# Three weight units of the first MLP, narrowed over six items instead of three

## The chip, the cores and the metric

One core of a Trainium2 chip runs the kernel. The metric is the device time of one execution in microseconds (us). The engines are TensorE (PE, matmuls), VectorE (DVE), ScalarE (ACT), GpSimd (POOL) and SyncE (SP, which here issues most of the DMAs). Each engine works through its own queue in the order in which the program was written.

## The reference

Pooled attention feeds an MLP with squared ReLU, whose result is routed to the best of eight experts. The change lies in the first MLP.

```python
q_pool = q.reshape(B, H, S // 2, 2, D).mean(axis=3)
attn = softmax(scale * q_pool @ k.T); attn_out = attn @ v     # 2 x 8 heads, 1152 keys, D = 64
x = attn_out.transpose(0, 2, 1, 3).reshape(1152, 512)
h = x @ w_in                      # 512 x 2048, float64 weights
r = np.maximum(h, 0.0)
x = (r * r) @ w_out               # 2048 x 512, float64 weights
...                               # gate, top 1 of 8 experts, capacity 288: relu(x @ w1[e]) @ w2[e]
```

## The kernel before

**The MLP.** The 1152 tokens are cut into 3 blocks of 384 (`tb`) and the 2048 hidden columns into 2 halves (`hf`) of 8 blocks of 128 (`f`). An *item* is one `(hf, tb, f)`; there are 48, numbered from 0, in that order of loops. `g1` of an item makes the first product into a bank `bs` (L939, 12 matmuls: four blocks of the 512 inputs times three products of high and low parts), ACT makes `r` from it with Relu (L948) and the high part `gh` of its square (L950), DVE squares `r` (L952) and subtracts `gh` to get the low part `gl` (L954). `g2` makes the second product from these (L968, 9 matmuls: three blocks of 128 tokens, each with `gh` times the high weights, `gh` times the low weights, `gl` times the high weights). PE does `g1` of item n and then `g2` of item n - 2. The first product of item 0 is already made at the end of the attention stage. From item to item two `bs` banks, two `r` buffers and three pairs `gh`, `gl` take turns.

**The weights.** They arrive as float64. One *unit* is 256 hidden columns, of `w_in` or of `w_out`, so each unit serves two values of `f`. Eight pairs make 16 units; those numbered 0 to 7 are of the first half `hf`: units 0, 2, 4, 6 are `w_in` and 1, 3, 5, 7 are `w_out`. A unit is loaded raw (`ops[0]`, 1 MB, L157 or L162), narrowed to float32 by three DVE instructions of 128 x 1024 each on its bits (L171, L177, L183), and then split: a high part is copied out (L206 on POOL or L204 on ACT) and DVE subtracts it to make the low part (L210 of `split_lo`). There are two raw buffers: unit 6 has one to itself, units 5 and 7 share the other, so the load of unit 7 waits until L183 of unit 5 has read it. Units 0 to 4 are made during the attention stage, the last of them on POOL (L206 and L210) just as the items begin. Units 5, 6 and 7 are made beside the first items. Their users are `g2` of item 4 for unit 5, `g1` of item 6 for unit 6, and `g2` of item 6 for unit 7.

**The order around the items.** The kernel is scheduled by hand: an engine's queue has the order of the code. `mat(n, f, front)` puts a piece of work beside item n. In item n the program writes `g1` of item n, then the work of front 1, then `g2` of item n - 2 (from n = 2 on), then the work of front 2 (the default) and 3. The work at n = -1 comes before item 0.

```python
    for n in range(NI):
        g1(*items[n])
        for f in mtodo.pop((n, 1), []):
            f()
        if 2 <= n < NI - 1:
            g2(*items[n - 2])
        for x in (2, 3):
            for f in mtodo.pop((n, x), []):
                f()
```

In the kernel before, unit 5 is narrowed beside item 0, unit 6 beside item 1 and unit 7 beside item 2, and each is split at the next item's front 1.

Of the kernel before, what the change touches and what calls it, by code (L numbers as in the profile page):

```python
# [21 lines left out]
def tile_pooled_attention__relu2_mlp__top1_experts(  # L22
# [122 lines left out]
    wf = {}  # L145
# [54 lines left out]
    def split_hi(key, src, eng_hi="pool"):  # L200
        hi, lo = slots.take(), slots.take()
        halves[key] = (hi, lo)
        if eng_hi == "act":
            nc.scalar.activation(out=hi, in_=src, func=AF.Copy)  # L204
        else:
            nc.gpsimd.tensor_scalar(out=hi, in0=src, scalar1=1.0, scalar2=0.0, op0=ALU.mult, op1=ALU.add)  # L206

    def split_lo(key, src, eng=None, hold=False):
        hi, lo = halves[key]
        (eng or nc.vector).tensor_tensor(out=lo, in0=src, in1=hi.bitcast(F32), op=ALU.subtract)  # L210
        if not hold:
            stage.give(src)

    def split(key, src, eng_hi="pool", eng_lo=None, hold=False):
        split_hi(key, src, eng_hi)
        split_lo(key, src, eng_lo, hold)
# [11 lines left out]
    pool = att.enter_context(tc.tile_pool(name="scores", bufs=1, space=PSUM))  # L228
# [293 lines left out]
    for w in range(5):  # L522
        ops = nwork.pop(0)
# [460 lines left out]
    def mat(n, f, front=2):  # L984
        mtodo.setdefault((n, front), []).append(f)
# [2 lines left out]
    PB = NTB * FH  # L988
    for w, key in enumerate(units[5:8]):
        ops = nwork.pop(0)  # L990
        mat(-1 if w < 2 else 0, ops[0])
        for u, f in enumerate(ops[1:]):
            mat(w, f, 1 + (u == 2))
        mat(w + 1, lambda key=key, w=w: split(key, wf[key], "act" if w == 1 else "pool"), 1)
    assert KX >= 2 * XTW
    grow = [af[:, KU + i * UW : KU + (i + 1) * UW] for i in range(NGROW)]
    early = 7
# [11 lines left out]
    for j in range(HI):  # L1009
        for u, kind in enumerate(("in", "out")):  # L1010
            key = (kind, HI + j)
# [416 lines left out]
```

## Time and profile before

| | us |
|---|---|
| median of 3 runs | 596.58 (596.32 to 598.05) |
| profiled execution, its own time | 597.89 |
| its span, first to last instruction | 596.1 |
| PE busy | 572.1 (96%) |
| DVE busy | 338.7 (57%) |
| ACT busy | 260.8 (44%) |
| POOL busy | 168.7 (28%) |

The busy times are sums over the whole span; the stages differ, so what matters for a change in one stage is the stretch in which it lies. The attention stage ends at about 234 us, the items run from there to about 440 us, the experts follow.

### The profile page before, as it was taken

How to read it: one execution, taken by the hardware profiler on the slowest of the kernel's cores; microseconds unless marked ns; L12 is line 12 of the kernel's file. 1: busy time of each engine (PE TensorE's matmuls, PEld its weight loads, DVE VectorE, ACT ScalarE, POOL GpSimd, SP SyncE). 2: the span in 40 equal slices, each digit the busy share in tenths (PEclk: the TensorE clock that was granted, in tenths of full speed). 3: DMA queues.
4: the chain of work that ended last, by engine and by line, in shares of the span. 5: the costliest groups of instructions: out<-in, count | busy, mean ns of one | idle time of the engine just before them, and what ended most of it. 6: DMA issues, size and time to landing. Idle time of an engine off the chain costs nothing. (4 is left out here: it accounts for less than half of the span.)

```text
span 596.1 us, 13050 instructions
## 1 busy us (share of the span) xinstructions
PE 572.1 (96%) x5309; PEld 443.1 (74%) x5309; DVE 338.7 (57%) x550; ACT 260.8 (44%) x552; POOL 168.7 (28%) x274
## 2 busy tenths in 40 slices
PE   8999999999999999889999999999998997989994
PEld 4788889888888878778989999888886453444342
DVE  4889798888888784956569932335354110111110
ACT  5787878787877765223232322323432111010110
POOL 3746457575636253300014200001022121000011
PEclk9999999999999999999999999999999998999998
DMA  8674964417343003121344780001066940999400
GB/s 203 186 232 149 313 222 150 108 55 196 79 120 112 3 6 139 70 73 73 140 141 134 264 308 1 0 2 45 0 232 244 286 110 23 378 346 361 159 8 15
DMA packets 37639, 84.72 MB, mean 142 GB/s; under 512 B 4225, under 2 KB 8837, under 8 KB 37568
## 3 DMA queue, kind: packets, MB, share of 16 engines
q1 hardware_dynamic: 35824, 80.71, 42.3%
q0 software_dynamic: 1376, 2.81, 1.3%
q8 instruction: 47, 0.77, 0.5%
q10 hardware_dynamic: 368, 0.23, 0.2%
q14 instruction: 24, 0.20, 0.1%
HBM read 73.83 MB, written 11.37 MB: 143 GB/s over the span
## 5 line engine op out<-in xcount | busy, mean ns | idle before, releaser
L939 PE MATMUL bs<-ax,gs 128*128 128x384 f32 x564 | 107.1, 338 | 0.4 <-ACT af L496 0.4
L376 DVE TENSOR_REDUCE nm<-sc 128x1 f32<-128x1152 f32 x72 | 97.3, 1354 | 11.3 <-ACT af L437 4.0
L939 PEld LDWEIGHTS bs<-ax,gs 128*128 128x128 f32 x564 | 99.7, 188 | 5.2 <-issue 1.2
L968 PE MATMUL bt<-gs,gg 128*128 128x512 f32 x360 | 94.1, 397 | 3.4 <-DVE gg L954 3.4
L367 PE MATMUL sc<-gs 64*128 64x384 f32 x576 | 94.3, 363 | 0.0
L384 ACT ACTIVATE af<-sc,nm 128x1152 f32<-128x1152 f32 x72 | 87.7, 1218 | 9.7 <-DVE nm L376 9.4
L968 PEld LDWEIGHTS bt<-gs,gg 128*128 128x128 f32 x360 | 66.4, 188 | 16.9 <-DVE gg L954 4.7
L948 ACT ACTIVATE af<-bs 128x384 f32<-128x384 f32 x47 | 23.1, 492 | 120.7 <-PE bs L939 117.6
L367 PEld LDWEIGHTS sc<-gs 64*128 64x128 f32 x576 | 65.0, 187 | 7.3 <-issue 3.4
L952 DVE TENSOR_TENSOR af<-af 128x384 f32<-128x384 f32 x48 | 28.5, 593 | 72.6 <-ACT af L948 71.9
L411 PE MATMUL bm<-ident,af 64*128 64x64 f32 x576 | 50.5, 226 | 1.0 <-DVE af L435 0.5
L411 PE MATMUL ba<-ident,af 64*128 64x64 f32 x576 | 49.9, 227 | 0.6 <-DVE af L435 0.3
L411 PEld LDWEIGHTS bm<-ident,af 64*128 64x128 f32 x576 | 43.2, 138 | 9.3 <-DVE af L435 4.1
L206 POOL TENSOR_SCALAR gs<-af 128x1024 fp32r<-128x1024 f32 x15 | 20.2, 1347 | 85.6 <-PE bs L939 66.2
L435 DVE COPY af<-bm 128x512 f32<-128x512 f32 x56 | 38.2, 682 | 10.1 <-PE ba L411 7.7
L411 PEld LDWEIGHTS ba<-ident,af 64*128 64x128 f32 x576 | 41.3, 139 | 1.5 <-DVE af L435 0.6
L437 ACT ACTIVATE af<-ba 128x512 f32<-128x512 f32 x56 | 33.3, 595 | 20.0 <-PE ba L411 15.3
L738 POOL DMA_INDIRECT disp<-af,rslot x9 | 9.2, 1018 | 95.3 <-DVE rslot L900 60.8
L473 PE MATMUL ba<-af,gx 128*64 128x128 f32 x576 | 35.0, 275 | 0.7 <-ACT af L437 0.6
L473 PEld LDWEIGHTS ba<-af,gx 128*64 128x64 f32 x576 | 31.1, 137 | 5.6 <-ACT af L437 3.6
L473 PE MATMUL ba<-af 128*64 128x128 f32 x576 | 35.0, 275 | 0.1
L473 PEld LDWEIGHTS ba<-af 128*64 128x64 f32 x576 | 31.1, 137 | 5.0 <-ACT af L437 3.0
(208 smaller groups left out, 850.0 us busy)
## 6 DMA issues: line engine op xcount, KB each, us to landing
af<-in_moe_w_dram SPq DMA_DIRECT2D x32, 512.0 KB, 8.2
gf<-in_moe_w_dram SPq DMA_DIRECT2D x30, 512.0 KB, 7.4
af<-in_moe_w_in_dram SPq DMA_DIRECT2D x8, 1024.0 KB, 5.4
af<-in_moe_w_out_dram SPq DMA_DIRECT2D x8, 1024.0 KB, 4.9
af<-in_q_dram SPq DMA_DIRECT2D x28, 288.0 KB, 4.8
disp<-af SPq DMA_DIRECT2D x6, 771.0 KB, 6.9
af<-in_k_dram SPq DMA_DIRECT2D x12, 192.0 KB, 4.2
af<-in_v_dram SPq DMA_DIRECT2D x4, 576.0 KB, 5.4
```

Source lines behind the costliest of these rows:

```text
L206: nc.gpsimd.tensor_scalar(out=hi, in0=src, scalar1=1.0, scalar2=0.0, op0=ALU.mult, op1=ALU.add)
L367: inst = nc.tensor.matmul(S_[part_, bank, :KS], lhsT=lhs[rows2[r]], rhs=rhs[rows2[r], kc], start=(m == 0), stop=(m == len(groups_) - 1),)
L376: inst = nc.vector.tensor_reduce(out=nm, in_=bank_sets[n % 2][:, :, :KS], axis=AX.XY, op=ALU.max, negate=True)
L384: inst = nc.scalar.activation(out=prs[n % NPB].rearrange("p (i s) -> p i s", i=3), in_=bank_sets[n % 2][:, :, :KS], func=AF.Exp, bias=st.p ...
L411: nc.tensor.transpose(views[:, m, :], x, ident[rows2[i], rows2[i]])
L435: nc.vector.tensor_copy(out=dst, in_=src)
L437: nc.scalar.activation(out=dst, in_=src, func=AF.Copy)
L473: inst = nc.tensor.matmul(av[rows2[h], :w], lhsT=vs[p % 2][:, h, c * D : (c + 1) * D], rhs=of(c, h), start=(c == 0), stop=(c == NKC - 1),)
L939: nc.tensor.matmul(ph[:, :TB], lhsT=w[:, cw], rhs=x[:, d, tb * TB : (tb + 1) * TB], start=(n == 0), stop=(n == 3 * NDC - 1),)
L948: nc.scalar.activation(out=r, in_=ph[:, :TB], func=AF.Relu)
L952: nc.vector.tensor_tensor(out=g, in0=r, in1=r, op=ALU.mult)
L968: nc.tensor.matmul(accs[tb][t], lhsT=g[:, ct], rhs=w[:, cw], start=(f == 0 and n == 0), stop=(f == FH - 1 and n == 2),)
```

## The change

The loop over units 5, 6 and 7 (`w` = 0, 1, 2) places its pieces elsewhere.

```diff
     for w, key in enumerate(units[5:8]):
         ops = nwork.pop(0)
-        mat(-1 if w < 2 else 0, ops[0])
         for u, f in enumerate(ops[1:]):
-            mat(w, f, 1 + (u == 2))
-        mat(w + 1, lambda key=key, w=w: split(key, wf[key], "act" if w == 1 else "pool"), 1)
+            mat(2 * w + (u > 0), f, 1 + (u == 2))
+        mat(-1 if w < 2 else 1, ops[0])
+        mat(2 * w + 2, lambda key=key: split(key, wf[key], "act"))
```

Each unit now has two items: L171 beside the first, L177 and L183 beside the second, and the split after that, at front 2 of items 2, 4 and 6. The load of unit 7 is written at item 1, behind L183 of unit 5, instead of at item 0. All three high parts are made on ACT (L204); before, units 5 and 7 had theirs on POOL (L206). The queue of SP and the order of PE's instructions are the same as before.

On DVE, at the beginning of the items, the queue before reads as follows, from the low part of item 0 (`gg` holds `gh` and `gl`, `af` holds raw and narrowed weights and `r`, `gs` the split weights).

```order
L954 TENSOR_TENSOR gg<-af,gg 128x384
L171 TENSOR_SCALAR af<-af 128x1024
L177 SCALAR_TENSOR_TENSOR af<-af 128x1024
L183 SCALAR_TENSOR_TENSOR af<-af 128x1024
L952 TENSOR_TENSOR af<-af 128x384
L954 TENSOR_TENSOR gg<-af,gg 128x384
L210 TENSOR_TENSOR gs_75<-af,gs_75 128x1024
L171 TENSOR_SCALAR af<-af 128x1024
L177 SCALAR_TENSOR_TENSOR af<-af 128x1024
L183 SCALAR_TENSOR_TENSOR af<-af 128x1024
L952 TENSOR_TENSOR af<-af 128x384
L954 TENSOR_TENSOR gg<-af,gg 128x384
```

A whole unit stands ahead of L952 and L954 of each item. In the changed kernel, from the same place:

```order
L954 TENSOR_TENSOR gg<-af,gg 128x384
L171 TENSOR_SCALAR af<-af 128x1024
L952 TENSOR_TENSOR af<-af 128x384
L954 TENSOR_TENSOR gg<-af,gg 128x384
L177 SCALAR_TENSOR_TENSOR af<-af 128x1024
L183 SCALAR_TENSOR_TENSOR af<-af 128x1024
L952 TENSOR_TENSOR af<-af 128x384
L954 TENSOR_TENSOR gg<-af,gg 128x384
L171 TENSOR_SCALAR af<-af 128x1024
L210 TENSOR_TENSOR gs_75<-af,gs_75 128x1024
L952 TENSOR_TENSOR af<-af 128x384
L954 TENSOR_TENSOR gg<-af,gg 128x384
```

L952 and L954 of item 1 now have one instruction of unit 5 ahead of them instead of three, and L171 of the next unit stands ahead of L210 of the one before.

On ACT the difference between the two kernels is this piece of the queue, from item 2 on (its Relu from the second `bs` bank, L948, and its square, L950, come first).

```order
 L948 ACTIVATE af<-bs_3879 128x384
 L950 ACTIVATE gg<-af 128x384
-L948 ACTIVATE af<-bs_3878 128x384
-L950 ACTIVATE gg<-af 128x384
-L948 ACTIVATE af<-bs_3879 128x384
-L950 ACTIVATE gg<-af 128x384
+L204 ACTIVATE gs_75<-af 128x1024
+L948 ACTIVATE af<-bs_3878 128x384
+L950 ACTIVATE gg<-af 128x384
+L948 ACTIVATE af<-bs_3879 128x384
+L950 ACTIVATE gg<-af 128x384
+L204 ACTIVATE gs_75<-af 128x1024
```

Ahead of this piece one L204 stands in both kernels, behind item 2: of unit 6 before, of unit 5 in the changed kernel. The two that are added stand behind item 4 and behind item 6.

## Rows read from the trace of the kernel before

**Rows 1.** Windows: length, busy us by engine (instructions), PE clock, DMA share, GB/s.

```profile
230.00:260.00 30.00, 25.61 (x195) 22.67 (x192) 23.96 (x28) 8.59 (x20) 11.31 (x18) 1.00 0.19 60
260.00:300.00 40.00, 40.00 (x201) 36.04 (x200) 23.18 (x32) 11.79 (x23) 0.00 (x0) 1.00 0.25 89
```

**Rows 2.** PE's waits from 225 us on: total us, times, longest.

```profile
PE bt L968 <- DVE gg L954: 3.4, 3, 1.7
PE bt L1165 <- PEq L1302: 2.4, 1, 2.4
```

**Rows 3.** Timeline of PE: start, us, what, idle before.

```profile
240.99 2.27 PE L939 MATMUL bs<-ax,gs 128*128 128x384 f32 x12
243.10 0.63 PE L968 MATMUL bt<-gs,gg 128*128 128x512 f32 x2
244.56 1.91 PE L968 MATMUL bt<-gs,gg 128*128 128x512 f32 x7 [0.83 <-DVE gg L954]
246.31 2.25 PE L939 MATMUL bs<-ax,gs 128*128 128x384 f32 x12
...
251.69 2.26 PE L939 MATMUL bs<-ax,gs 128*128 128x384 f32 x12
...
257.81 2.25 PE L939 MATMUL bs<-ax,gs 128*128 128x384 f32 x12
...
282.99 2.27 PE L939 MATMUL bs<-ax,gs 128*128 128x384 f32 x12
```

**Rows 4.** Timeline of DVE beside the first items.

```profile
236.85 0.82 DVE L171 TENSOR_SCALAR af<-af 128x1024 uint32<-128x1024 uint32 x1
...
239.68 2.91 DVE L183 SCALAR_TENSOR_TENSOR af<-af 128x1024 uint32<-128x1024 uint32 x1
...
243.25 1.25 DVE L954 TENSOR_TENSOR gg<-af,gg 128x384 fp32r<-128x384 f32 x1
...
249.34 0.56 DVE L954 TENSOR_TENSOR gg<-af,gg 128x384 fp32r<-128x384 f32 x1
249.89 1.23 DVE L210 TENSOR_TENSOR gs<-af,gs 128x1024 fp32r<-128x1024 f32 x1
251.03 0.69 DVE L171 TENSOR_SCALAR af<-af 128x1024 uint32<-128x1024 uint32 x1
251.75 1.23 DVE L177 SCALAR_TENSOR_TENSOR af<-af 128x1024 uint32<-128x1024 uint32 x1
253.01 1.23 DVE L183 SCALAR_TENSOR_TENSOR af<-af 128x1024 uint32<-128x1024 uint32 x1
254.16 0.55 DVE L952 TENSOR_TENSOR af<-af 128x384 f32<-128x384 f32 x1
254.84 1.18 DVE L954 TENSOR_TENSOR gg<-af,gg 128x384 fp32r<-128x384 f32 x1
```

**Rows 5.** Timeline of ACT: the one high part that it makes.

```profile
248.80 1.06 ACT L204 ACTIVATE gs<-af 128x1024 fp32r<-128x1024 f32 x1 [8.64 <-DVE af L183]
```

**Rows 6.** Timeline of POOL; last, line 210 alone: ns shortest/median/longest.

```profile
237.09 1.49 POOL L206 TENSOR_SCALAR gs<-af 128x1024 fp32r<-128x1024 f32 x1
238.66 2.85 POOL L210 TENSOR_TENSOR gs<-af,gs 128x1024 fp32r<-128x1024 f32 x1
...
243.06 1.04 POOL L206 TENSOR_SCALAR gs<-af 128x1024 fp32r<-128x1024 f32 x1
254.40 1.22 POOL L206 TENSOR_SCALAR gs<-af 128x1024 fp32r<-128x1024 f32 x1 [10.30 <-DVE af L183]
...
L210 POOL TENSOR_TENSOR gs<-af,gs x5: 1996/2000/2847, 93.9 to 238.7; 128x1024 fp32r<-128x1024 f32 x5
```

**Rows 7.** Load of unit 7 on SP; DMA issues 215 to 300 us: KB, landing.

```profile
242.62 0.37 SPq L162 DMA_DIRECT2D af<-in_moe_w_out_dram  x1
...
af<-in_moe_w_out_dram SPq DMA_DIRECT2D x4, 1024.0 KB, 4.9
```

**Rows 8.** Window behind the branch of L1302, columns as in group 1.

```profile
502.37:509.00 6.63, 6.52 (x14) 3.60 (x15) 0.00 (x0) 1.07 (x2) 0.00 (x0) 0.50 0.39 126
```

## The prediction

> **What bounds the kernel now.** I read the windows first. From 260 us on PE is busy for all of its 40.00 us and VectorE (DVE) for 23.18 of them, so PE is the bound there; from 230 to 260 us PE is busy for 25.61 of 30 us and DVE for 23.96 [rows 1]. This second stretch holds the first MLP items. PE's waits come next. From 225 us to the end the largest is 3.4 us in three pieces, always the second product (L968) waiting for `gl`, the low part that DVE makes at L954; no DMA is among PE's longer waits, so what PE gains in the MLP should reach the end [rows 2].
>
> PE's own timeline gives the price. An undisturbed item takes 4.197 us: item 6 begins at 257.81 and item 12 at 282.99, 25.18 us for six. The first product of item 3 begins at 240.99 and that of item 6 at 257.81, 16.82 us where three items should take 12.59 [rows 3]. So **4.23 us** are lost, 0.81 more than the 3.42 us of bare gaps (three times 0.27 us for getting under way again).
>
> DVE's rows tell why. One unit costs DVE, from start to start, 0.72 (L171), 1.26 (L177), 1.15 (L183) and 1.14 (L210), 4.27 us, and one item 0.68 (L952) plus 0.55 (L954), 1.23 us [rows 4]. A unit in every item is 5.5 us against PE's 4.2: the queue of DVE falls behind. POOL adds to it. L183 at 239.68 took 2.91 us beside POOL's L210, while it takes 1.23 at 253.01; L954 at 254.84 took 1.18 [rows 4, 6].
>
> **The change, step by step.** It adds no arithmetic. Two high parts go from POOL's L206 (1.04 us) to ScalarE's L204 (1.06 us) [rows 5, 6]; ACT is busy for 8.59 of the 30 us [rows 1], so both are covered there. The 12 DVE instructions of the units stay and are spread: 4.27 + 2 x 1.23 = 6.73 us for two items against 8.39 us of PE. That removes the backlog, if the order meets PE's due times. I place them with item k's first product at 240.99 + 4.197 (k - 3) and the second product that follows 2.11 us later (243.10 - 240.99) [rows 3]; its third matmul, which reads `gl`, about 0.5 us on.
>
> *Item 1.* L171 begins at 236.85 as before. L952 and L954 of item 1 now come right behind it, but POOL works for the earlier unit at that time: L206 from 237.09 to 238.58, then L210 to 241.51 [rows 6]. Unhindered, they are done at 236.85 + 0.72 + 0.68 + 0.55 = 238.8. At the other end each waits for POOL: L183 ended 1.08 us after POOL's L210 (242.59 against 241.51) [rows 4, 6], which gives 242.6. I take a point between: L954 at 243.25 ended 0.40 us after L206 on POOL did (244.50 against 244.10) [rows 4, 6], so L952 ends at 238.98, POOL's L210 then runs its usual 2.00 us to 240.98, L954 ends at 241.4. PE wants this `gl` at 243.6: met in all three cases.
>
> [...]
>
> *The tight place.* Behind L954 of item 1, DVE works through L177, L183, item 2, L171 of the second unit, L210 of the first, item 3, L177, L183, item 4, L171 of the third unit, and then L210 of the second: 2 x 1.26 + 2 x 1.15 + 3 x (0.68 + 0.55) + 2 x 0.72 + 1.14 = 11.09 us, and 1.23 for that last L210 itself [rows 4]. From 241.4 it is done at 253.7. Its low part is a weight of item 6, whose first product begins at 240.99 + 12.59 = 253.58 and reads it in its third matmul, two twelfths of 2.11 us later, at 253.93. So it is 0.2 us early; from 238.8 it is 2.8 us early, from 242.6 it is 1.0 us late and costs 1.0 + 0.27 = 1.3 us. I take no stall, the price by the middle.
>
> *The rest is not tight.* `gl` of items 2, 3 and 4 comes at about 245.1, 248.1 and 251.8, PE wants it at 247.8, 252.0 and 256.2. L204 stands in ACT's queue ahead of the next item's L948 and L950, as it did when ACT sat idle 8.64 us for it [rows 5]; the first now runs at 243.9 to 245.0 while item 3's product is there at 243.1, and PE wants that bank back at 249.4, 4 us of cover. The second runs at about 250.9 to 251.9, 0.4 us past the end of item 5's product, whose `gl` has 5 us. The third unit's L210 ends near 260, PE wants its result at 264. The load of the third unit still waits for the first unit's L183, 242.59 before and 243.9 now; landing takes 4.9 us [rows 7], so 248.8, and its L171 is due at 251.8: 3.0 us of cover. POOL only loses work, and the two short instructions behind it come earlier.
>
> **The sum.** 4.23 us removed, nothing added. The profiled execution took 597.89 us for a span of 596.1; it would be 593.7 for a span of 591.9. It lies 1.31 us above the median of the runs shown (596.58), so the median becomes 596.58 - 4.23 = **592.4 us**. About 0.3%, 1.8 us, is what a measurement of this kernel can tell from no change.
>
> **The rivals.**
>
> *The stall moves instead of going.* If POOL holds DVE longer than in any row, or the low part misses item 6 and the backlog passes on to the next, half of the loss stays: 596.58 - 2.1 = 594.5. For it speaks the slack of 0.2 us; against it that DVE has 1.66 us to spare in every two items, so a miss is made good within one unit.
>
> [...]
>
> *Slower: the third load holds DVE.* Its L171 now stands ahead of the second unit's L210 in DVE's queue, and item 6 needs that L210; before, nothing of item 6 was behind it. Each us that the load lands after 251.8 delays PE by one. The time passes that of before when the stall is above 4.23 us, and is slower by more than 0.3% from 6.0 us: the low part ready at 259.9, the load landed at about 258.0, 14 us after its issue where the row says 4.9 [rows 7]. The DMA engines are busy for only 0.19 of this stretch [rows 1], which speaks against it. At the point where it decides the time is 598.4.
>
> **How the numbers follow.** The forecast has 0.70; with the stall of the tight place left between 0 and 1.3 us, and about a microsecond of spread below, its own range is 591.2 to 593.7. The stall that moves has 0.08 (594.5, half of it inside 0.3%). The clock has 0.17: 0.07 for 590.7 or less, 0.06 for 594.1, 0.04 for 595.7. The load that holds DVE, or anything like it, has 0.05, of which 0.03 slower. Faster by over 0.3% means below 594.8: 0.70 + 0.04 + 0.13 = 0.87, of which I keep 0.86; the same 0.11, slower 0.03. A range from 590.7 to 594.8 leaves out some 0.15.
>
> **What would show it.** In the changed kernel's profile the wait of L968 for L954 should be gone, and items 3 to 6 should begin at 241.0, 245.2, 249.4 and 253.6, 4.2 us apart. DVE's L210 of the second unit should end between 251 and 254.2; if PE's L939 waits for it, by how much shows the tight place. L204 should appear three times, near 244, 251 and 258. All of PE's later rows should lie 4.2 us earlier. The prediction is wrong if items 3 to 6 are not 4.2 us apart, or if they are and the span does not follow, in which case the 6.63 us at 0.50 are the first place to look.

## The result, and the profile after

The changed kernel took **591.53 us** (median of 4 executions, 589.70 to 593.33) against 596.63 us before (4 executions): ratio 0.9907, 95% interval 0.9879 to 0.9936. Twelve more executions, beside 29 more of the kernel before, gave 592.54 against 596.20 us, ratio 0.9940 (0.9922 to 0.9959). The forecast was 592.4 us with a range from 590.7 to 594.8. The ratios in this document are the estimates on record, with their intervals; they are not quite the quotients of the medians. The profiled execution took 593.33 us for a span of 591.6.

The windows of the changed kernel, columns as in [rows 1], show the stretch of the first items filled.

```profile
230.00:260.00 30.00, 29.02 (x221) 26.52 (x220) 23.39 (x30) 12.04 (x24) 7.81 (x16) 1.00 0.15 42
260.00:300.00 40.00, 40.00 (x201) 36.23 (x201) 22.70 (x32) 11.79 (x23) 0.00 (x0) 1.00 0.36 128
```

PE is busy for 29.02 instead of 25.61 us of the first 30 [rows 1]. DVE has about as much to do there as before, 23.39 against 23.96 us. Of PE's waits from 225 us on, the longest that is left is the gap at the branch; L968 waiting for L954 is not in the list any more [rows 2].

```profile
PE bt L1165 <- PEq L1302: 2.4, 1, 2.4
PE bt L1204 <- ACT ar L1197: 1.0, 2, 0.5
```

PE's timeline: the first products of items 3 to 7.

```profile
241.94 2.27 PE L939 MATMUL bs<-ax,gs 128*128 128x384 f32 x12
...
246.14 2.27 PE L939 MATMUL bs<-ax,gs 128*128 128x384 f32 x12
...
250.34 2.27 PE L939 MATMUL bs<-ax,gs 128*128 128x384 f32 x12
...
254.54 2.27 PE L939 MATMUL bs<-ax,gs 128*128 128x384 f32 x12
...
258.74 2.27 PE L939 MATMUL bs<-ax,gs 128*128 128x384 f32 x12
```

They lie 4.20 us apart, where [rows 3] had 5.32, 5.38 and 6.12. All of it is 0.95 us later than I placed it, because the attention stage ended 0.95 us later in this execution.

DVE's timeline of the same stretch: item 1 after L171, then the three L210, of units 5, 6 and 7.

```profile
238.57 1.37 DVE L952 TENSOR_TENSOR af<-af 128x384 f32<-128x384 f32 x1
240.04 2.17 DVE L954 TENSOR_TENSOR gg<-af,gg 128x384 fp32r<-128x384 f32 x1
...
246.39 1.22 DVE L210 TENSOR_TENSOR gs<-af,gs 128x1024 fp32r<-128x1024 f32 x1
...
252.84 1.22 DVE L210 TENSOR_TENSOR gs<-af,gs 128x1024 fp32r<-128x1024 f32 x1
...
258.88 1.22 DVE L210 TENSOR_TENSOR gs<-af,gs 128x1024 fp32r<-128x1024 f32 x1
```

On POOL, L206 and L210 of unit 4 run beside the first two of these rows.

```profile
238.03 1.49 POOL L206 TENSOR_SCALAR gs<-af 128x1024 fp32r<-128x1024 f32 x1
239.61 2.18 POOL L210 TENSOR_TENSOR gs<-af,gs 128x1024 fp32r<-128x1024 f32 x1
```

L952 ends at 239.94, 0.42 us behind POOL's L206, and L954 at 242.21, 0.42 us behind POOL's L210: it takes 2.17 us where it takes 0.56 alone. ACT's three high parts:

```profile
244.77 1.06 ACT L204 ACTIVATE gs<-af 128x1024 fp32r<-128x1024 f32 x1 [3.67 <-DVE af L183]
...
251.20 1.06 ACT L204 ACTIVATE gs<-af 128x1024 fp32r<-128x1024 f32 x1 [1.69 <-DVE af L183]
...
257.81 1.04 ACT L204 ACTIVATE gs<-af 128x1024 fp32r<-128x1024 f32 x1
```

**Where the time came from, and what is chance.** One profiled execution of each kernel can be cut into stretches by PE's timeline: from the start to the first L939 (attention); from there to the first product of the experts, L1188 (the items and the routing); and from the first L1165 behind the gap at L1302 to the first L1253 (the work just behind that branch).

| kernel | start to first L939 | first L939 to first L1188 | L1165 to L1253 behind the gap |
|---|---|---|---|
| before | 234.63 | 221.25 | 11.18 |
| changed | 235.58 | 216.99 | 9.58 |
| changed, again | 234.98 | 217.03 | 8.34 |

PE's rows behind the first two lines of the table, before:

```profile
234.63 4.43 PE L939 MATMUL bs<-ax,gs 128*128 128x384 f32 x24 [0.38 <-ACT af L496]
455.88 3.65 PE L1188 MATMUL bs<-af,ar 128*64 128x512 f32 x16
502.37 1.73 PE L1165 MATMUL bt<-ident,af 128*128 128x128 f32 x8 [2.41 <-PEq L1302]
513.55 1.59 PE L1253 MATMUL bt<-ident,ar 128*128 128x128 f32 x8
```

Changed:

```profile
235.58 4.43 PE L939 MATMUL bs<-ax,gs 128*128 128x384 f32 x24 [0.38 <-ACT af L496]
452.57 3.65 PE L1188 MATMUL bs<-af,ar 128*64 128x512 f32 x16
499.08 1.64 PE L1165 MATMUL bt<-ident,af 128*128 128x128 f32 x8 [2.43 <-PEq L1302]
508.66 1.59 PE L1253 MATMUL bt<-ident,ar 128*128 128x128 f32 x8
```

The stretch of the items is 4.26 and 4.22 us shorter; the others differ between two executions of the changed kernel itself.

### The profile page after: what moved, and what is told of

Same layout as the page of the kernel before. It is cut to its first block, busy times and chain, and to the rows that moved or that the text cites. A ratio compares the mean times of both kernels' runs of the same rounds, so it can differ in the third digit from the quotient of the medians.

```text
span 591.6 us, 13045 instructions
## 1 busy us (share of the span) xinstructions
PE 568.6 (96%) x5309; PEld 442.1 (75%) x5309; DVE 338.3 (57%) x550; ACT 262.9 (44%) x554; POOL 165.1 (28%) x272
## 3 DMA queue, kind: packets, MB, share of 16 engines
q0 software_dynamic: 1376, 2.81, 1.3%
## 5 line engine op out<-in xcount | busy, mean ns | idle before, releaser
L939 PE MATMUL bs<-ax,gs 128*128 128x384 f32 x564 | 107.1, 338 | 0.4 <-ACT af L496 0.4
L939 PEld LDWEIGHTS bs<-ax,gs 128*128 128x128 f32 x564 | 99.7, 188 | 5.2 <-issue 1.2
L968 PE MATMUL bt<-gs,gg 128*128 128x512 f32 x360 | 93.2, 396 | 0.0
L968 PEld LDWEIGHTS bt<-gs,gg 128*128 128x128 f32 x360 | 66.7, 188 | 12.4
L948 ACT ACTIVATE af<-bs 128x384 f32<-128x384 f32 x47 | 23.1, 493 | 117.6 <-PE bs L939 117.6
L952 DVE TENSOR_TENSOR af<-af 128x384 f32<-128x384 f32 x48 | 30.1, 626 | 68.9 <-ACT af L948 68.0
L206 POOL TENSOR_SCALAR gs<-af 128x1024 fp32r<-128x1024 f32 x13 | 17.8, 1370 | 76.9 <-PE bs L939 62.7
```

Of the source, the lines that this page charges most:

```text
L939: nc.tensor.matmul(ph[:, :TB], lhsT=w[:, cw], rhs=x[:, d, tb * TB : (tb + 1) * TB], start=(n == 0), stop=(n == 3 * NDC - 1),)
L948: nc.scalar.activation(out=r, in_=ph[:, :TB], func=AF.Relu)
L952: nc.vector.tensor_tensor(out=g, in0=r, in1=r, op=ALU.mult)
L968: nc.tensor.matmul(accs[tb][t], lhsT=g[:, ct], rhs=w[:, cw], start=(f == 0 and n == 0), stop=(f == FH - 1 and n == 2),)
```

## The experiments

**The change once more, in more executions.** No edit.

> The changed kernel itself, in more executions. In the first profile of it the MLP items take 4.26 us less than before (from the first L939 to the first L1188: 216.99 against 221.25 us); the rest of the difference lies in the attention stage (0.95 us later) and behind the branch of L1302 (1.6 us shorter), which differ from execution to execution of one kernel. Theory (only the 4.2 us are the change's): the median lies 4.2 us under that of before, within 1 us, ratio about 0.993. Rival (the first measured 5.1 us are the change's): ratio about 0.9915 and below.

Measured: 592.54 us, ratio 0.9940 (0.9922 to 0.9959), 3.7 us by the medians. The items took 217.03 us. The first theory holds: 4.2 us (0.993) lie inside this interval, the rival's 0.9915 lies just outside it. So the 5.1 us of the first medians were 4.2 us and some luck.

**The spread alone, on POOL.**

```diff
-        mat(2 * w + 2, lambda key=key: split(key, wf[key], "act"))
+        mat(2 * w + 2, lambda key=key, w=w: split(key, wf[key], "act" if w == 1 else "pool"))
```

> The spread over six items alone: units 5 and 7 have their high parts on POOL again (L206), as before the change. Theory (the backlog of DVE was the cause, and the spread removes it): L206 of unit 5 holds L954 of item 2 for at most 1 us, which eats the room of 0.8 us at item 6; items 3 to 6 begin 4.2 us apart except for at most 0.4 us at item 6, and the median is 591.5 to 592.0. Rival (POOL's work beside DVE was the cause, and the move to ScalarE is what helped): PE waits 1.3 us or more between items 3 and 7, and the median is above 592.8.

Measured: 593.40 us against 596.74, ratio 0.9937 (0.9915 to 0.9959). By the median this is the rival's side, and the theory's 591.5 to 592.0 is missed, but PE's timeline shows no wait in the items:

```profile
251.80 2.27 PE L939 MATMUL bs<-ax,gs 128*128 128x384 f32 x12
253.91 2.25 PE L968 MATMUL bt<-gs,gg 128*128 128x512 f32 x9
256.00 2.27 PE L939 MATMUL bs<-ax,gs 128*128 128x384 f32 x12
258.10 2.25 PE L968 MATMUL bt<-gs,gg 128*128 128x512 f32 x9
260.19 2.27 PE L939 MATMUL bs<-ax,gs 128*128 128x384 f32 x12
```

Items 5, 6 and 7 begin 4.20 us apart, and the stretch of the items is 216.97 us. This execution began its items at 237.04 and took 10.04 us behind the gap, which is where its own time went; of the others only the time is known. DVE's low part of unit 6:

```profile
254.94 1.22 DVE L210 TENSOR_TENSOR gs<-af,gs 128x1024 fp32r<-128x1024 f32 x1
```

It is done at 256.16, 0.2 us before item 6's third matmul wants it (256.00 + 0.35); L954 of item 2 took 1.21 us beside POOL's L206, as the theory had it. Because of the median I ran this kernel again beside the changed one.

> The spread over six items alone, with the high parts of units 5 and 7 on POOL, beside the changed kernel on one chip. Theory (ScalarE adds nothing while no wait of PE is left): the same as the changed kernel within 1 us, and the stretch of the items 217.0 us long in both. Rival (the first medians, 593.4 and 591.5 us, tell a cost of POOL's work): slower than the changed kernel by 1.5 us or more, with a longer stretch of the items.

Measured: 592.76 us, ratio 0.9959 (0.9939 to 0.9979), beside 592.54 us of the changed kernel; the stretch of the items is 217.07 against 217.03. The two differ by 0.2 us in the median, and their intervals overlap. ScalarE adds no time that these runs can tell once the units are spread; what it adds is room, 0.8 us instead of 0.2 in front of item 6.

**The move to ScalarE alone.** The edit is made to the kernel before.

```diff
-        mat(w + 1, lambda key=key, w=w: split(key, wf[key], "act" if w == 1 else "pool"), 1)
+        mat(w + 1, lambda key=key, w=w: split(key, wf[key], "act"), 1)
```

> The move to ScalarE alone: one unit beside each of items 0 to 2 as before, all three high parts on ACT. Theory (backlog): L954 of items 1 and 3 lose their 0.69 and 0.62 us beside L206 of POOL, the three stalls of PE stay, and the loss of 4.23 us shrinks to about 3.0 us; the median is about 595.4. Rival (ScalarE is what helped): the loss is under 1 us and the median below 593.

Measured: 594.73 us, ratio 0.9976 (0.9953 to 0.9998). Two of the three stalls stay, and the first shrinks: item 4 begins 4.60 us after item 3, 0.40 us too late. PE's timeline:

```profile
240.56 2.27 PE L939 MATMUL bs<-ax,gs 128*128 128x384 f32 x12
...
248.82 1.89 PE L968 MATMUL bt<-gs,gg 128*128 128x512 f32 x7 [0.93 <-DVE gg L954]
250.55 2.27 PE L939 MATMUL bs<-ax,gs 128*128 128x384 f32 x12
252.65 0.63 PE L968 MATMUL bt<-gs,gg 128*128 128x512 f32 x2
254.33 1.90 PE L968 MATMUL bt<-gs,gg 128*128 128x512 f32 x7 [1.04 <-DVE gg L954]
256.06 2.26 PE L939 MATMUL bs<-ax,gs 128*128 128x384 f32 x12
```

Item 3 begins at 240.56 and item 6 at 256.06, 15.50 us where 12.59 would do: 2.91 us are lost, 3.0 were expected, and the stretch of the items is 219.95 us. So of the 4.26 us the move alone brings 1.30, and the spread alone brings all of them; they don't add up.

**A later low part for item 6.**

```diff
             mat(2 * w + (u > 0), f, 1 + (u == 2))
+            if w == 1 and u == 2:
+                mat(3, f)
+                mat(3, f)
```

> The changed kernel with L183 of unit 6 done three times (the result is the same, the instruction sets bits that are set already): 2.5 us more on DVE ahead of the low part of unit 6. In the changed kernel that low part is ready at 254.06 us and the third matmul of item 6 would take it at 254.89, so 0.83 us are free. Theory (this place is the tight one, and a miss costs its length and 0.27 us): PE's first product of item 6 waits for DVE's L210 for 1.7 us, its start to the next one's grows by 2.0 us, the median is about 593.5. Rival (the spare time of DVE takes it up, nothing on PE's path): no wait, 591.5.

Measured: 594.02 us, ratio 0.9951 (0.9930 to 0.9973). PE's timeline, the first products of item 5, item 6 (in two rows, around the wait) and item 7:

```profile
250.30 2.27 PE L939 MATMUL bs<-ax,gs 128*128 128x384 f32 x12
...
254.79 0.61 PE L939 MATMUL bs<-ax,gs 128*128 128x384 f32 x2
256.60 2.02 PE L939 MATMUL bs<-ax,gs 128*128 128x384 f32 x10 [1.20 <-DVE gs L210]
258.46 2.25 PE L968 MATMUL bt<-gs,gg 128*128 128x512 f32 x9
260.55 2.27 PE L939 MATMUL bs<-ax,gs 128*128 128x384 f32 x12
```

Item 5 began at 250.30, so item 7 was due at 258.70 and came at 260.55: 1.85 us are lost, of 2.52 us that were put in. DVE's rows of the repeated instruction and of the low part:

```profile
249.90 3.75 DVE L183 SCALAR_TENSOR_TENSOR af<-af 128x1024 uint32<-128x1024 uint32 x3
...
255.33 1.22 DVE L210 TENSOR_TENSOR gs<-af,gs 128x1024 fp32r<-128x1024 f32 x1
```

The low part was done at 256.55, where 256.58 was expected. Item 6's third matmul was due at 250.30 + 4.20 + 0.35 = 254.85 and ran at 256.60, 1.75 us late, where 1.7 was expected. The idle time in its row is only 1.20 us, because the two matmuls ahead of it began at 254.79 instead of 254.50 and took longer too; why, the rows don't show. The place is the tight one, and its room in the changed kernel is 2.52 - 1.75, about 0.8 us.

**Unit 7 loaded behind unit 6.**

```diff
-    nwork = [narrow_ops(kind, g, u == 6) for u, (kind, g) in enumerate(units)]
+    nwork = [narrow_ops(kind, g, u in (6, 7)) for u, (kind, g) in enumerate(units)]
...
-        mat(-1 if w < 2 else 1, ops[0])
+        mat(-1 if w < 2 else 3, ops[0])
```

> The changed kernel with unit 7 loaded into the raw buffer of unit 6, behind L183 of that unit, instead of the buffer of unit 5: its load goes out at about 251.2 us instead of 244.8. Theory (L171 of unit 7 holds the queue of DVE until the load has landed, and L210 of unit 6 stands behind it): landing at 256.1, the low part of unit 6 at 257.9, PE waits 3.0 us in item 6 and loses 3.3; the median is about 594.8. Rival (the load stays covered): no wait, 591.5.

Measured: 598.40 us, ratio 1.0042 (1.0013 to 1.0070), slower than before. DVE's row of unit 7 and the low part of unit 6 behind it:

```profile
255.64 0.70 DVE L171 TENSOR_SCALAR af<-af 128x1024 uint32<-128x1024 uint32 x1 [4.12 <-DMA af<-in_moe_w_out_dram]
256.25 1.22 DVE L210 TENSOR_TENSOR gs<-af,gs 128x1024 fp32r<-128x1024 f32 x1
```

PE's timeline from item 6 on:

```profile
257.52 2.36 PE L939 MATMUL bs<-ax,gs 128*128 128x384 f32 x10 [3.27 <-DVE gs L210]
259.68 3.51 PE L968 MATMUL bt<-gs,gg 128*128 128x512 f32 x9
263.03 2.25 PE L939 MATMUL bs<-ax,gs 128*128 128x384 f32 x12
```

The mechanism is as expected, the price is not: PE waits 3.27 us, but item 7 comes 5.10 us late (263.03 instead of 257.93, that is 8.40 us behind item 5, which began at 249.53), and the stretch of the items is 222.12 us. The nine matmuls of L968 took 3.51 us where they take 2.25. The windows behind the wait, the granted clock third from the end, tell why.

```profile
257.52:259.00 1.48, 1.48 (x8) 1.48 (x9) 1.35 (x4) 0.00 (x0) 0.00 (x0) 1.00 0.09 32
259.00:262.50 3.50, 3.50 (x11) 2.93 (x10) 3.33 (x5) 2.08 (x3) 0.15 (x1) 0.51 0.00 0
```

From 259.0 to 262.5 us the granted clock is 0.51 of full speed. By an estimate from these two numbers that costs half of 3.5 us, 1.75, which with the wait of 3.27 makes 5.02 of the 5.10 us. The other executions point the same way: the mean granted clock of this kernel's ten is 0.979 to 0.992, that of the changed kernel's twelve 0.992 to 0.998. In which stretch the nine without a profile lost it is not shown.

**Work for PE at the gap.** Two runs put 20 matmuls of 128 x 256 bf16, whose result is not used, on PE; the first right ahead of the first branch of the experts, the second at the end of the arm that expert 0 runs.

```diff
     complete(half - 1)
+    for _ in range(20):
+        nc.tensor.matmul(bank_m[:, : 2 * P], lhsT=upper, rhs=ident.bitcast(BF16), start=True, stop=True)
     for e in range(half):
```

> The changed kernel with 20 matmuls of 128 x 256 bf16 into a bank that nobody reads, written on PE right ahead of the first branch of the experts, some 2.1 us of work whose result is not used. [...] Rival (PE comes to the branch only when its queue is empty): the gap of 2.4 us stays, 2.1 us are added, and the clock falls as before; the median is 1.5 to 2.5 us above the changed kernel.

Measured: 595.19 us, ratio 0.9984 (0.9966 to 1.0003). It told nothing on the gap: the matmuls ran at 486.09, ahead of the branch into the arm, where PE doesn't stand, and the gap that ends at 500.81 was as long as ever (2.62 us). The median lies 2.65 us above the changed kernel, about what the added matmuls take (2.36 us in this profile; the 2.1 us was my estimate, and no row gives it). It was my misplacing. The second run:

```diff
         base_out(bank_m, yr[0], 2)
+        for _ in range(20):
+            nc.tensor.matmul(bank_t[3][:, : 2 * P], lhsT=upper, rhs=ident.bitcast(BF16), start=True, stop=True)
```

> The changed kernel with the 20 unused matmuls at the end of the arm that expert 0 runs, so that they lie right ahead of PE's gap at L1302; in the run before they lay ahead of the branch into that arm, 12 us earlier, where PE has no gap. Theory (the jump out of the arm waits for PE's own last matmul, so nothing that is queued on PE can cover it): a gap of 1.9 to 2.6 us stays behind the 20 matmuls, the time from the gap to the first L1253 is 8.4 us or up to 2.8 us longer as in the other runs, and the median is about 2.3 us above that of the changed kernel, 594.9. Rival (the 20 matmuls run while PE's sequencer is at the jump): the gap shrinks by 2 us, L1253 follows in 8.4 us, and the median is at or below that of the changed kernel, 592.5.

Measured: 595.42 us, ratio 0.9982 (0.9955 to 1.0008). PE's timeline:

```profile
495.48 2.36 PE L1287 MATMUL bt<-ident,upper 128*128 128x256 bf16 x20
500.65 1.73 PE L1165 MATMUL bt<-ident,af 128*128 128x128 f32 x8 [2.81 <-PEq L1304]
502.48 9.38 PE L1238 MATMUL bs<-gf,ar 128*128 128x512 f32 x16
```

The gap stays, at 2.81 us, behind the 20 matmuls, and L1253 follows 11.05 us after L1165. In this profile queued work does not cover the jump, so no version better than the changed kernel came of it.

## Why the prediction was right

**What bounds.** Right. The stretch of the items became 4.26 and 4.22 us shorter in the two profiles where 4.23 was worked out, and PE is the bound in it now.

**The backlog as the cause.** That the spread is what takes the stalls away is shown from both sides: without the move to ScalarE it leaves none (216.97 and 217.07 us for the items), and the move without the spread leaves 2.91 of the 4.23 us. What a unit in every item would have cost by itself is not shown. Before the change DVE was behind in item 1 already: beside POOL's L206 and L210 of unit 4 its L177 took 1.94 us and its L183 2.91, where each takes 1.23 for unit 7 [rows 4, 6]:

```profile
237.70 1.94 DVE L177 SCALAR_TENSOR_TENSOR af<-af 128x1024 uint32<-128x1024 uint32 x1
...
242.51 0.64 DVE L952 TENSOR_TENSOR af<-af 128x384 f32<-128x384 f32 x1
```

By the prediction's prices L952 would have begun at 239.98, 2.5 us earlier, and L954 then took another 0.7 beside POOL's L206 of unit 5 (1.25 us; 0.56 in the run of the move alone, without that L206). Without any of this, by an estimate from the same prices, `gl` of items 1, 2 and 3 would have come at 241.2, 246.7 and 252.2, where PE wants them at 243.6, 247.8 and 252.0: a wait of 0.2 us instead of three. By this estimate POOL used up DVE's lead first, and only then did DVE's pace of 5.5 us for each item become waits; the spread leaves room for both. No run took unit 4's work away from POOL, so how the 4.23 us divide stays open.

**Item 1 beside POOL.** The point between was right: L952 ends 0.42 us after POOL's L206, POOL's L210 follows (2.18 us, 2.00 assumed), L954 ends at 242.21, 241.26 when the 0.95 us of the later start are taken off; 241.4 was worked out. The four instructions end in turn, at 239.52 (L206), 239.94 (L952), 241.79 (L210) and 242.21 (L954), so L952 was done 1.85 us ahead of POOL's L210. Why they end in turn, the rows don't show. Of the 2.91 us that L183 took before the change, 1.83 lay beside POOL's L210 (239.68 to 241.51) and 1.08 came after it had ended, where the whole L183 took 1.23 at 253.01 [rows 4, 6].

**The tight place.** Right as a place, its room mis-sized: the low part of unit 6 was done at 254.06, that is 253.1 instead of 253.7. Each L171 took 0.60 or 0.61 us to the start of L210 behind it, not 0.72, and the items' pairs L952 and L954 took 1.13 to 1.16 us, not 1.23. The room is 0.8 us by the rows and by the run that took it away, not 0.2. With the room of 0.2 a small error would have brought a stall, so the choice of no stall rested on a margin that was larger than the prediction knew.

**Nothing else tight.** Right. The first L204 ran at 244.77 and the last ended at 258.85, and no wait of PE came from them. The load of unit 7 went out at 244.76 and its L171 did not wait.

**The sum.** 592.4 us was worked out from the median of before; the first four executions gave 0.9 us less, twelve more gave 592.54. What differs between the profiles beside the items' stretch differs between two executions of the changed kernel too.

**The rivals.** The stall that moves did not come. The third load as a cause of a slower kernel is a real mechanism (598.4 us when it is made to happen), but its price was too low: I counted one us for each us of delay, and a wait of 3.27 us cost 5.10, with the granted clock at 0.51 for 3.5 us behind it. The chances that the forecast gives to the clock at the branches stand at 590.7, 594.1 and 595.7 us, 1.7 us below and above the sum and 3.3 above it, and 590.7 is the lower end of the range too; 3.3 is an estimate, half of the 6.63 us at 0.50 before the change [rows 8], 1.7 is half of that, and no run shows a time that moved by these terms. What the runs show is that the granted clock behind the branch differs between executions of one kernel: 0.82 from L1165 to L1253 in the first profile of the changed kernel, and 1.00 from 490 to 520 us, which holds that work, in the second. The kernels that only the items tell apart took these times from L1165 to L1253: before 11.18, changed 9.58 and 8.34, POOL 10.04 and 8.35, ScalarE alone 9.75, late low part 8.35, late load 10.04. Executions of one kernel lie up to 1.7 us apart in these profiles, and the two extremes are 2.84 us apart. Nothing ties this to the change: the mean granted clock of a whole execution is 0.995 in the median for both kernels, 0.991 to 0.998 in the 29 of before and 0.992 to 0.998 in the 12 of the changed one. The profile of before that the prediction read had 0.990, below all of these. Both medians, 591.53 and 592.54 us, lie in the narrower range that the forecast had by itself, 591.2 to 593.7; single executions of the changed kernel went from 589.70 to 596.26.

## What to carry to other kernels

Where an in-order engine feeds the bound engine and has a batch of extra work, compare its work per step with the bound engine's step, and count the time for which a third engine holds it up: here L954 took 2.17 us beside POOL's L210 and 0.56 in the items behind. A batch that needs 5.5 us beside a step of 4.2 eats the lead that the engine has, and what comes after that are waits; spreading it so that it fits in every step removed them here without moving any work to another engine. Price a wait from start to start of the steps around it, not by the bare gap: three gaps of 3.42 us cost 4.23, and one of 1.20 cost 1.85. And before a difference of some 0.2% between two kernels is explained, cut their profiles into stretches and look whether it lies in the one that was changed.

## What the runs showed of the hardware that was not expected

A wait of 3.27 us in the stream of matmuls cost 5.10. The three waits of up to 1.7 us before the change left the granted clock at 1.00 [rows 1], and behind the one of 1.20 us the nine matmuls of L968 took their usual 2.25 us, while the one of 3.27 us was followed, 1.5 us after PE had started again, by 3.5 us at a granted clock of 0.51. Only one profile has a wait of that length in the items.

The gap at the jump out of expert 0's arm is 1.9 to 2.8 us long in these profiles. After gaps of 1.91 (late low part), 1.93 (changed, again) and 2.15 us (POOL, again) the work behind took 8.34 to 8.35 us, and the granted clock from 490 to 520 us, which holds it, was 1.00; after 1.92 (late load), 2.30, 2.40 and 2.62 us it took 9.75 to 10.04, and 9.58, 11.05 and 11.18 after 2.43, 2.81 and 2.41. Of these seven, six show a granted clock of 0.89 to 0.94 from 490 to 520 us; in the work itself it was 0.70 before the change and 0.82 in the first profile of the changed kernel. For the 11.05 us no window shows it. So gaps of 1.92 and 1.93 us were followed by 10.04 and 8.34 us: the length of the gap alone does not decide it. What else does, these runs don't show.
